# First rows of two experts loaded one step earlier in a fused HGRN2 and MoE kernel

## The chip, the cores and the metric

The kernel runs on one core of one Trainium2 chip. The time is the device time of one execution in microseconds, and the number given for a kernel is the median of several runs. A profiled execution gives the trace that is read here; its span is close to that time but not the same number.

The engines are named as in the profile: PE is TensorE (PEld its weight loads), DVE is VectorE, ACT is ScalarE, POOL is GpSimd, SP is SyncE, which here only issues DMAs.

## The reference

Two blocks follow one another. The first is a gated linear recurrence over 768 steps for 4 batches of 8 heads, with head size 48. The second is a mixture of 8 experts: each of the 3072 tokens goes to the one expert with the highest gate value, through a two-layer network of that expert, and is weighted by its gate probability. No token is dropped.

```python
# q, k, v, f_logit: (4, 8, 768, 48)
f = 1.0 / (1.0 + np.exp(-f_logit))
for t in range(S):
    state = f[:, :, t, :, None] * state + np.einsum('bhd,bhe->bhde', k[:, :, t], v[:, :, t])
    y[:, :, t] = np.einsum('bhd,bhde->bhe', q[:, :, t], state)
...
x = y.transpose(0, 2, 1, 3).reshape(3072, 384)
logits = x @ w_gate                    # (3072, 8)
expert_idx = np.argmax(logits, axis=1)
gate_w = softmax(logits)[arange, expert_idx]
...
for e in range(8):                     # rows of expert e
    h = np.maximum(x_sorted[lo:hi] @ w1[e], 0.0)     # w1: (8, 384, 1024)
    y_sorted[lo:hi] = h @ w2[e]                      # w2: (8, 1024, 384)
return gate_w[:, None] * y_sorted[inv_perm]
```

## The kernel before

**The recurrence.** It is cut into 12 units (NU = 12). A unit is one chunk of 128 time steps of two batches, all heads: 256 tokens. The loop at line 765 runs steps n = 1 to 13 as a software pipeline. In step n, unit n has its scores computed, unit n - 1 its output products, and unit n - 2 is copied out (`settle`), transposed together with the gate product (`rows`, tile `xp`, line 625) and laid into rows of a token-major tile `xr` (`lay`).

**Routing.** Finished units are routed in groups: [0,1], [2,3], [4,5], [6,7], [8,9], [10], [11]. `choose` finds each token's expert on VectorE. `count` is two small TensorE products (lines 220 and 221) that count tokens by expert. `place` (lines 227 to 245, VectorE) adds the counts to the running ends of the experts' regions and gives each token its row number `posi`. `fill` (lines 252 to 254) writes the gate weight. `send` then scatters the rows to the DRAM table `xs` by indirect DMAs from GpSimd (line 183), one for each 128 tokens. Each expert has its own region in `xs`, filled from its front in the order of routing. `settled` does place and fill, and queues the sends; a group of two units has four scatters, which go out two in each of the next two steps. `scatter_some` issues them. From step 10 on it issues all that are waiting: group [6,7] is settled in step 10 and its four scatters go out in that step, group [8,9] and [10] in step 12, group [11] in step 13.

**The early tiles.** Once an expert has 128 rows, its first full tile can be computed while the last units are still being routed. This is done for experts 0 and 1 (EARLY = 2). `load_rows` reads the tile from `xs` (four blocks at line 267, and the token numbers and gate weights `tg` at line 278, ten DMAs for the two experts, all on SyncE's queue). `turn` transposes it by VectorE (line 288). `widen` is the first layer on TensorE (line 304), with its ReLU on ScalarE (line 314) or VectorE (line 316), and `narrow` the second layer (line 320, tile `yp`), weighted by the gate at line 331 and scattered to the output. The tile of expert 0 is turned in step 12, and its first layer runs in pieces between the last products of the routing in steps 12 and 13. The tile of expert 1 follows after the loop.

**The test for full tiles.** If experts 0 and 1 do not have 128 rows each when the tile is loaded, the early tile would be wrong. Lines 713 to 720 therefore compare the running ends with `full` and write a flag `fix`, which at the end of the program would run a general loop over all experts (line 1106). The test is made when the group that is the last one before the loads is settled.

**Order.** All engines are under a hand-written order (`manual_schedule`): each engine runs its instructions in the order in which the program records them. The framework adds the waits for data. For `xs` it knows only the table as a whole: scatters do not wait for each other (they are declared free of conflicts), but a load of rows waits for every scatter recorded before it, and a scatter recorded after a load waits until that load has landed. A wait holds up everything behind it in its engine's own order, DMA issues on SyncE's queue too.

**After the loop**, the remaining rows of each expert are computed in tiles of up to 384 rows (`rows_of`, `narrow_late`), with rows beyond that collected in groups of four experts (`widen_quad`). The weights of expert 0 and 1 are loaded in steps 8 and 10 (lines 350 and 355), 1.5 MB for each tensor.

Of the kernel before, what the change touches and what calls it, by code (L numbers as in the profile page):

```python
# [25 lines left out]
NU = B // 2 * NC  # L26
# [28 lines left out]
EARLY = 2  # L55
# [64 lines left out]
def kernel(  # L120
# [22 lines left out]
    def const(name):  # L143
        a, w = fat[name]
        return fpack[:, a : a + w]
# [49 lines left out]
    class Route:  # L195
# [60 lines left out]
        def send(self, chunks):  # L256
            for c in chunks:
                scatter(xs, self.posi[:, c : c + 1], self.xr[:, c, :], ROWS - 1, self.group)
# [5 lines left out]
    def load_blocks(to, rows):  # L264

        for j in range(128 // BK):
            nc.sync.dma_start(
                to[BK * j : BK * j + BK],
                rows[:, DB * j : DB * j + DB].rearrange("(i c) m -> c i m", c=BK),
            )  # L270

    def load_rows(row, n=1):

        rows = xs[ds(row, n * C)] if not isinstance(row, int) else xs[row : row + n * C]
        x = rowp.tile([128, TILES * C // BK, DB], F32, name="xrow")[:, 0 : n * C // BK]
        tg = rowp.tile([128, TILES, USED - TOK], F32, name="tg")[:, 0:n]
        load_blocks(x, rows)
        nc.sync.dma_start(tg, rows[:, TOK:USED].rearrange("(t p) r -> p t r", p=C))
        return {"n": n, "x": x, "tg": tg}
# [58 lines left out]
    first = [e * REGION for e in range(E)]  # L338
# [44 lines left out]
    with ExitStack() as st:  # L383
# [85 lines left out]
        def by_r(u, part=whole, on=nc.gpsimd):  # L469
            k = units[u]["k"][:, part]  # L470
            ins = on.tensor_tensor(k, k, units[u]["r"][:, part], op=OP.mult).ins  # L471
            if routed:

                tc.add_manual_dep(ins, routed.pop().name, SYNC, reason="the port of both")

        def ends(u):
            nc.gpsimd.tensor_copy(rend[:, u], units[u]["sum"][:, :, C])
# [21 lines left out]
        def score(u, a):  # L499
            x = units[u]  # L500
            x["at"] = scores[u % 2]
            ps = x["ps", a] = [pss.tile([128, HP, C], F32, name="s") for h in range(2)]
            for p, h, r in heads():
                s = HP * a + p
                nc.tensor.matmul(  # L505
                    ps[h][:, p], lhsT=x["k"][r, s], rhs=x["q"][r, s], start=True, stop=True
                )
# [15 lines left out]
        def keep(u):  # L523
            for a in range(2):
                nc.scalar.copy(units[u]["kn"][:, HP * a : HP * a + HP], units[u]["kp"][a])  # L525
# [65 lines left out]
        def settle(u):  # L591
            x = units[u]
            x["ys"] = wk.tile([128, 2, HP, C], F32, name="ys", bufs=1)
            for a in range(2):
                nc.scalar.copy(x["ys"][:, a], x["yt"][:, a])  # L595
# [112 lines left out]
        def settled(n, rt):  # L708

            rt.place()  # L710
            rt.fill()
            lead["base"] = rt.after
            if n == NU - 3:
                lack = wk.tile([1, EARLY], F32, name="lack", bufs=1)
                some = wk.tile([1, 1], F32, name="some", bufs=1)
                nc.vector.tensor_tensor(
                    lack, rt.after[0:1, 0:EARLY], const("full")[0:1, 0:EARLY], op=OP.is_lt
                )
                nc.vector.reduce_max(some, lack, axis=AX_X)
                nc.vector.tensor_copy(fix, some)  # L720
            if n < NU:
                for c in range(0, rt.n, 2):
                    sends.append(lambda c=c: rt.send(range(c, c + 2)))
            else:
                rt.send(range(rt.n))
# [3 lines left out]
        def scatter_some(n):  # L729
            now = sends if n >= NU - 1 else sends[:1]  # L730
            for send in now:
                send()
            del sends[: len(now)]
# [31 lines left out]
        for n in range(1, NU + 2):  # L765
            here, back, last = n, n - 1, n - 2
            ahead = n + 1 < NU
            state = n < NU - 2
            rt = None
            if here < NU:  # L770
                units[here]["old"] = states[here % 2]
            if 1 <= last:
                settle(last)
            if later and later[0] < NU - 1:
                later[1].weigh()
            if here < NU:
                for a in range(2):
                    score(here, a)
            if ahead and n != 2:
                by_r(n + 1)  # L780
                ends(n + 1)
            if decayed:
                decayed()
                decayed = None
            if sends:
                scatter_some(n)
            if n == 1:
                units[0]["old"] = None
                added(0)
                update(0)()  # L790
            if ahead and n != 2:
                decay(n + 1)
                last_decay(n + 1)
            if state:
                keys(here)
                keep(here)
            if n == 2:
                growth(n + 1)
                by_r(n + 1)
                ends(n + 1)  # L800
                decay(n + 1)
                last_decay(n + 1)
            if here < NU:
                for a in range(2):
                    for h in range(2):
                        mask(here, a, h)
            if n == 1:
                log(3)
            if n + 3 < NU:
                steps(n + 3)  # L810
            if later and n >= NU - 1:
                settled(*later)
                later = None
                scatter_some(NU)
            if 2 < n < NU - 2:
                total(n + 2)
            if n == NU - 2:
                by_decay(n + 1)
            if 0 <= last:
                rt = rows(last, later[1] if later else None)  # L820
                lay(last)
            if later and n == NU - 2:
                settled(*later)
                later = None
                scatter_some(NU)
            if ahead and n < NU - 2:
                by_decay(n + 1)
            if n == 2:
                total(n + 2)
            if rt:  # L830
                rt.choose()
                if n < NU - 2:
                    routed.append(rt.latest)
                if n >= NU - 1:
                    rt.weigh()
            if later:
                settled(*later)
                routed.append(later[1].latest)
                later = None
            for a in range(2):  # L840
                if back < NU:
                    within(back, a)
            if n == 1:
                settle(0)
            if n + 2 < NU and n != 1:
                growth(n + 2)
            if n == NU + 1:
                widen(soon[0], weights[0], early_h, range(3, 7))
            if n == NU:
                turn_early(soon[0])  # L850
            if state:
                added(here)
                decayed = update(here)
            if n == 1:
                total(3)
            if back < NU:
                before(back)
            if rt:
                later = (n, rt)
                if n >= NU - 1:  # L860
                    rt.count(turns("rp", [128, 2, rt.n, E]))
                if n >= NU:
                    settled(*later)
                    later = None
            if n == NU:
                early_h = early_banks()
                widen(soon[0], weights[0], early_h, range(3))
            if n == NU + 1:
                widen(soon[0], weights[0], early_h, range(7, NF))
                turn(soon[1])  # L870
            if n == 1:
                load(n + 3, "q")
            if n + 3 < NU:
                load(n + 3, "k")
            if n + 2 < NU:
                load(n + 2, "v")
            if 1 < n and n + 3 < NU:
                load(n + 3, "q")
            if n + 5 < NU:
                load(n + 5, "f")  # L880
            if n == 1:
                load_first_pads()
            if n in (8, 10):
                load_first_weights((n - 8) // 2)
                load_second_weights((n - 8) // 2)
            if n == NU - 1:
                soon = [load_rows(first[e]) for e in range(EARLY)]


        def share():  # L890
# [368 lines left out]
```

## Time and profile before

| what | us |
|---|---|
| time, median of 3 runs | 409.92 (407.5 to 410.32) |
| span of the profiled execution | 410.9 |
| TensorE busy | 390.1 (95%) |
| VectorE busy | 170.6 (42%) |
| ScalarE busy | 102.9 (25%) |
| GpSimd busy | 112.3 (27%) |
| tiles of all experts, TensorE from 153.28 to 402.39 | 249.1 |

TensorE's share of 95% says that the kernel as a whole is bound by it, but the average hides that the stretches differ. The recurrence with its routing takes the first 130 us or so, then comes a short stretch in which routing ends and the early tiles run, and then the full tiles, which are nothing but matmuls. In the last part there is no wait left to take away. A wait in the middle stretch counts only if TensorE stands still for it.

Where the profile says "issue", the engine waited for nothing that the profile shows. "Remote" or "another core or an unknown queue" means that a semaphore changed at that time but the trace could not tie the change to the end of an instruction; on a kernel of one core it is not another core. In a windows table each engine has its busy time and its number of instructions, then follow the clock that was granted to TensorE (1.00 is full), the busy share of the DMA engines, and GB/s.

### The profile page before, as it was taken

Reading aid. Unit: us, or ns where it says so; the run is one execution under the profiler, and the core shown is the slowest. Engines: PE = TensorE matmul, PEld = TensorE weight load, DVE = VectorE, ACT = ScalarE, POOL = GpSimd, SP = SyncE. Lnnn points to the kernel's source line nnn. Section 1 sums busy time; section 2 is a strip of 40 time slices with the busy share of each in tenths; the row PEclk is TensorE's granted clock in tenths of the full one; section 3 lists DMA queues with packets and bytes.
Section 4 is the critical chain, followed back from the end, with each engine's and each line's share of the span. In section 5 each row is a group of like instructions: output and inputs, shape, how many; then the busy total and the mean of one; then the engine's idle time right before and its main releaser. Section 6 shows DMA issues by size and latency. Waiting matters only on the chain.

```text
span 410.9 us, 7299 instructions
## 1 busy us (share of the span) xinstructions
PE 390.1 (95%) x2870; PEld 272.1 (66%) x2870; DVE 170.6 (42%) x364; ACT 102.9 (25%) x190; POOL 112.3 (27%) x118
## 2 busy tenths in 40 slices
PE   7878999999999699999999999999999999999991
PEld 7878899989978478685555555545455555554540
DVE  6989888887752631212131131119112113111810
ACT  7888778675232001010100100110000000001000
POOL 5378667778705200000001001000200100100020
PEclk9998999999999699999999999999999999999997
DMA  8998667769953358785539999892172379994010
GB/s 291 406 359 296 213 213 256 237 200 360 404 156 105 121 157 282 176 294 109 185 108 396 362 384 332 322 352 31 51 255 83 97 252 383 405 406 169 1 46 17
DMA packets 52122, 95.22 MB, mean 232 GB/s; under 512 B 21440, under 2 KB 41333, under 8 KB 50032
## 3 DMA queue, kind: packets, MB, share of 16 engines
q1 hardware_dynamic: 48592, 84.96, 61.1%
q0 software_dynamic: 3200, 9.64, 6.3%
q8 instruction: 24, 0.39, 0.4%
q10 hardware_dynamic: 288, 0.08, 0.1%
q14 instruction: 18, 0.15, 0.1%
HBM read 79.65 MB, written 15.40 MB: 231 GB/s over the span
## 4 chain that ended last, share of the span: by engine, by line
PE 86%; DMA 4%; ACT 3%; DVE 2%; another core or an unknown queue 1%; issue 1%; SPq 0%; POOL 0%; POOLq 0%; ACTq 0%; DVEq 0%
PE yps L320 28%; PE hps L304 28%; PE xp L625 6%; PE yt L533 5%; PE s L505 4%; DMA f<-in_fu_dram 4%; PE yp L320 3%; PE yps L1059 3%; PE hps L1033 3%; PE yt L554 2%; PE s L304 2%; PE dp L570 2%; PE kp L520 1%; ACT g L438 1%
## 5 line engine op out<-in xcount | busy, mean ns | idle before, releaser
L320 PE MATMUL yps<-w2t,hT 128*128 128x384 f32 x352 | 115.6, 487 | 0.0
L304 PE MATMUL hps<-xT,w1t 128*128 128x384 f32 (+1 forms) x384 | 114.9, 459 | 0.0
L304 PEld LDWEIGHTS hps<-xT,w1t 128*128 128x128 f32 x384 | 73.0, 190 | 41.1
L320 PEld LDWEIGHTS yps<-w2t,hT 128*128 128x128 f32 x352 | 66.5, 190 | 48.1 <-issue 2.9
L183 POOL DMA_INDIRECT out_dram<-ysb,dst x26 | 25.3, 972 | 239.7 <-DVE ysb L331 239.4
L314 ACT ACTIVATE hT<-hps 128x384 f32<-128x384 f32 (+1 forms) x28 | 14.1, 505 | 209.7 <-PE hps L304 190.8
L316 DVE TENSOR_SCALAR hT<-hps 128x384 f32<-128x384 f32 (+1 forms) x28 | 16.2, 577 | 97.2 <-PE hps L304 97.2
L331 DVE TENSOR_SCALAR ysb<-yps,tg 128x384 f32<-128x384 f32 x22 | 13.6, 618 | 73.4 <-PE yps L320 73.4
L183 POOL DMA_INDIRECT xs<-xr,posi x24 | 30.9, 1289 | 22.3 <-issue 16.7
L511 DVE COPY_PREDICATED at<-mpack,s 128x512 f32<-128x512 uint8 x48 | 31.2, 727 | 11.9 <-PE s L505 10.3
L471 POOL TENSOR_TENSOR k<-k,r 128x1024 f32<-128x1024 f32 (+1 forms) x12 | 26.5, 2209 | 25.6 <-ACT r L467 9.9
L625 PE MATMUL xp<-fpack,ys 128*128 128x104 f32 x192 | 25.9, 286 | 4.6 <-ACT kn L525 3.7
L453 DVE TENSOR_TENSOR_SCAN sum<-g,cap 128x1032 f32<-128x1032 f32 (+1 forms) x14 | 28.7, 2051 | 2.7 <-ACT g L446 2.6
L625 PEld LDWEIGHTS xp<-fpack,ys 128*128 128x128 f32 x192 | 23.3, 196 | 6.9 <-ACT kn L525 4.9
L505 PE MATMUL s<-q,k 64*128 64x128 f32 x384 | 24.7, 278 | 1.6 <-POOL last L489 1.0
L533 PE MATMUL yt<-at,v 128*48 128x128 f32 x384 | 25.1, 282 | 0.6 <-issue 0.6
L505 PEld LDWEIGHTS s<-q,k 64*128 64x128 f32 x384 | 22.4, 188 | 3.5 <-issue 1.5
L533 PEld LDWEIGHTS yt<-at,v 128*48 128x48 f32 x384 | 21.3, 127 | 2.6 <-issue 1.6
L320 PE MATMUL yp<-w2t,hT 128*128 128x384 f32 x32 | 13.6, 584 | 3.3 <-DVE hT L316 3.3
L494 DVE TENSOR_TENSOR q<-q,g 128x1024 f32<-128x1024 f32 (+1 forms) x14 | 16.4, 1182 | 0.0
L595 ACT COPY ys<-yt 128x512 f32<-128x512 f32 x24 | 12.8, 587 | 13.8 <-PE yt L554 13.8
L288 DVE STREAM_TRANSPOSE xT<-xrow 128x1152 f32<-128x1152 f32 (+2 forms) x10 | 14.3, 1433 | 0.8 <-DMA xrow<-xs 0.7
(110 smaller groups left out, 324.6 us busy)
## 6 DMA issues: line engine op xcount, KB each, us to landing
qw<-in_moe_w_dram SPq DMA_DIRECT2D x16, 1536.0 KB
w1t<-in_moe_w_dram SPq DMA_DIRECT2D x8, 1536.0 KB
w2t<-in_moe_w_dram SPq DMA_DIRECT2D x8, 1536.0 KB
k<-in_ku_dram SPq DMA_DIRECT2D x12, 512.0 KB
q<-in_qu_dram SPq DMA_DIRECT2D x12, 512.0 KB
f<-in_fu_dram SPq DMA_DIRECT2D x11, 512.0 KB
xs<-pad SPq DMA_DIRECT2D x8, 600.0 KB
v<-in_vu_dram SPq DMA_DIRECT2D x12, 384.0 KB
```

Source lines behind the costliest of these rows:

```text
L183: ins = nc.gpsimd.indirect_dma_start(out=dst, out_offset=bass.IndirectOffsetOnAxis(ap=idx, axis=0), in_=src, in_offset=None, bounds_check= ...
L288: nc.vector.transpose(x["xT"].rearrange("p k (i c) -> p i k c", c=BK), x["x"].rearrange("p i (r k) -> p i k r", k=KD),)
L304: nc.tensor.matmul(x["h"][:, f], lhsT=w[0][:, j, b * 128 : b * 128 + 128], rhs=x["xT"][:, j], start=j == 0, stop=j == KD - 1,)
L316: nc.vector.tensor_scalar(to, x["h"], 0.0, None, op0=OP.max)
L320: nc.tensor.matmul(yp, lhsT=x["hT"][:, f, t * C : t * C + C], rhs=w[1][:, f, :], start=f == 0, stop=f == NF - 1,)
L453: nc.vector.tensor_tensor_scan(x["sum"][:, part].rearrange("p s c -> p (s c)"), x["g"][:, part].rearrange("p s c -> p (s c)"), cap[:, part ...
L471: ins = on.tensor_tensor(k, k, units[u]["r"][:, part], op=OP.mult).ins
L494: nc.vector.tensor_tensor(q, q, x["dec"][:, part], op=OP.mult)
L505: nc.tensor.matmul(ps[h][:, p], lhsT=x["k"][r, s], rhs=x["q"][r, s], start=True, stop=True)
L511: nc.vector.copy_predicated(x["at"][:, a, h], _bc(causal, 1, HP), x["ps", a][h])
L533: nc.tensor.matmul(x["yt"][DP * (h ^ a) : DP * (h ^ a) + D, a, p], lhsT=x["v"][:, a, 2 * p + h], rhs=x["at"][:, a, h, p], start=p == 0, st ...
L625: nc.tensor.matmul(xp[:, p], lhsT=x["ys"][:, a, p], rhs=wx[:, p, 0:XW] if a else wx[:, p, E:WX], start=True, stop=True,)
```

## The change

The loads of the first tiles of experts 0 and 1 move from the end of step 11 to the middle of step 10, right after that step's call of `scatter_some`. There the last scatters recorded before them are those of group [4,5], not [6,7]. So the test for full tiles, too, is taken one group earlier: with NU = 12, `n == NU - 3` is the group that is completed in step 9, [6,7], and `n == NU - 5` the one of step 7, [4,5]. The purpose is to issue the loads earlier, behind fewer scatters. The scatters of group [6,7], which stood before the loads in the program, now stand behind them, and so do the weight loads of expert 1 on SyncE's queue. TensorE, ScalarE and GpSimd have the same instructions in the same order as before; VectorE's three test instructions and SyncE's loads are the ones that move.

```diff
@@ settled(n, rt)
             lead["base"] = rt.after
-            if n == NU - 3:
+            if n == NU - 5:
                 lack = wk.tile([1, EARLY], F32, name="lack", bufs=1)
                 some = wk.tile([1, 1], F32, name="some", bufs=1)
                 nc.vector.tensor_tensor(
...
@@ the loop over n
             if sends:
                 scatter_some(n)
+            if n == NU - 2:
+                soon = [load_rows(first[e]) for e in range(EARLY)]
             if n == 1:
                 units[0]["old"] = None
                 added(0)
...
             if n in (8, 10):
                 load_first_weights((n - 8) // 2)
                 load_second_weights((n - 8) // 2)
-            if n == NU - 1:
-                soon = [load_rows(first[e]) for e in range(EARLY)]
```

## The prediction

> **What bounds the kernel now.** I read three views in this order: the chain of waits around the place of the change, the windows of that stretch, and the timelines of VectorE, the SyncE queue and GpSimd there. The chain first. From 153.28 us to 402.39 us it is TensorE alone (the windows give 249.08 us busy of 249.12), so nothing done before 150 us can help that part except by letting it start sooner. The only long piece of the chain that is not TensorE's after 37 us is this:
>
> ```profile
> 125.27 1.78 PE xp L625 x16
> 128.47 6.06 another core or an unknown queue
> 134.56 0.19 DVE counts L228
> 136.07 0.67 DVE hT L316
> 136.78 5.49 PE yp L320 x8
> ```
>
> The reader should see a VectorE instruction, the copy of group [11]'s counts at line 228, starting 6 us after its predecessor, then the place computation, then the hT that TensorE needs for the second half of `yp`. The windows show what this costs TensorE:
>
> ```profile
> core 0: us, PE busy (x) PEld busy (x) DVE busy (x) ACT busy (x) POOL busy (x), PEclk, DMA share, GB/s
> 109.20:115.00 5.80, 5.22 (x64) 4.32 (x60) 2.93 (x5) 0.72 (x2) 3.91 (x4) 1.00 1.04 390
> 130.69:133.44 2.75, 2.75 (x10) 1.33 (x8) 0.00 (x0) 0.00 (x0) 2.17 (x5) 1.00 0.41 149
> 133.44:136.78 3.34, 0.00 (x0) 0.00 (x0) 1.95 (x10) 0.00 (x0) 0.30 (x3) 0.86 0.16 61
> 136.78:142.69 5.91, 5.91 (x11) 3.48 (x12) 4.55 (x20) 0.00 (x0) 2.02 (x2) 0.50 0.52 176
> ```
>
> TensorE is idle for 3.34 us and then runs 5.91 us at a granted clock of 0.50. The timeline names the neighbours of that wait:
>
> ```profile
> 125.89 0.97 POOL L183 DMA_INDIRECT xs<-xr,posi  x1 [11.81 <-issue]
> 129.72 0.37 PE L221 MATMUL rp<-oh,fpack 128*128 128x16 f32 x2
> 132.51 0.97 POOL L183 DMA_INDIRECT xs<-xr,posi  x1 [0.31 <-issue]
> 133.60 0.14 POOL L617 MEMSET xr<- 128x28 f32 x1
> 134.56 0.17 DVE L228 COPY counts<-rp 128x16 f32<-128x16 f32 x1 [6.08 <-remote]
> ```
>
> The product that line 228 waits for has left TensorE at 130.09 (129.72 + 0.37). In the semaphore events kept in the trace, TensorE's increment for it arrives at 134.53, 4.4 us late. In that time GpSimd issues scatters one behind another: six from 125.89 to 133.48. The same lateness, 1.4 to 3.3 us, stands at 110.7 to 115.0, and there too GpSimd has a row of scatters (four, 109.27 to 114.08). Where it has only two together (95.33 and 96.68, for one) the increments come within 0.05 us. From one trace this is a coincidence in time, not a proven cause.
>
> Why six scatters stand together at 125.89: GpSimd was idle for 11.81 us before them, though the places of group [8,9] were ready at 119.2 (line 254: 119.01 + 0.18). The rows of `xs` that the early loads read must not be overwritten by a later scatter before they are read, so those scatters wait for all ten loads, and the loads came late:
>
> ```profile
> 99.91 0.46 SPq L350 DMA_DIRECT2D w1t<-in_moe_w_dram  x1
> 100.42 1.32 SPq L355 DMA_DIRECT2D w2t<-in_moe_w_dram  x1
> 118.35 1.76 SPq L267 DMA_DIRECT2D xrow<-xs  x4
> 120.63 2.44 SPq L267 DMA_DIRECT2D xrow<-xs  x4
> ```
>
> They were issued at 118.35, when the scatters of [6,7] (to 114.08) had landed, behind 3 MB of weights; they landed by 124.87.
>
> **What the Trainium skill says.** "DMA: Bandwidth & Descriptors", section Rules for kernel authors: a DMA that reads what an earlier one wrote must wait for that one's completion semaphore. The trace agrees: the queue waits 14.9 us at longest at line 267 for `xs<-xr,posi`. "Perfetto Trace Analysis", section DMA Instruction — SWDGE (GPSIMD): the recorded end of such a scatter is the end of descriptor generation, not of the movement. Agrees: 0.97 us recorded, 2.6 us at least to landing. "TensorE: Matmul & The Clock Gate", Part 1: an idle window of about 3.4 us halves TensorE's clock. Agrees: 3.34 us idle, then 0.50. The same page, section The cost: per-tile semaphore tail, gives 26.3 ns per increment; the 4.4 us here are nothing of that kind, so no price of the page covers them.
>
> **The change part by part.**
>
> *The test.* Three tiny VectorE instructions (lines 716, 719, 720: 0.12, 0.14 and 0.14 us, about 0.45 us with gaps) move from group [6,7], at 108.90, to group [4,5], at 91.6. There they precede the state addition of line 587 (0.54 us, whose next wait on TensorE has 1.34 us of idle time to absorb them). Cost nothing. The test asks whether experts 0 and 1 have 128 rows each by then. Counting the routing on the reference's inputs gives 238 and 207 after unit 5, so it still passes and the fallback loop stays unused; otherwise the kernel would be far slower.
>
> *The loads.* On the queue they now stand before the second expert's w1t and w2t and behind v, issued at 99.53. They wait for the second half of group [4,5]'s scatters, GpSimd 104.30 and 105.64. In the kernel before these landed at 111.26 and 112.35 among the weights' packets; those weights are now queued behind the loads. Low end: 2.6 us after 105.64, so 108.3; high end the old 112.35. I take 108.6. The ten loads then land 6.5 us later (118.35 to 124.87 before), at 115.1. They were needed at 121.07 (VectorE waits 0.74 us for them at line 288), so that wait goes, but behind it line 228 waits for TensorE's 123.17 in both kernels: worth 0.
>
> *The new wait.* Group [6,7]'s four scatters, issued at 109.27 before, must now wait for the loads: 115.1 plus the 1.02 us seen between 124.87 and 125.89, so 116.1. Behind them on GpSimd stand only scatters and the fills of lines 616 and 617; the last decay and state products are ahead of them. With one scatter each 1.28 us: [6,7] to 120.9, [8,9] to 126.0, [10] from 126.4 to 128.7. Before, [10] ended at 133.48. So GpSimd is behind by 7 us at first and ahead by 4.8 at the end. If the loads land only at 118.9 (high end), [10] ends at 132.5, still not later than before. Who waits for the scatters of [6,7]: ScalarE's first copy into the reused `xr` (126.41). With the old 5 to 7 us to landing under full queues they land at 125 to 127; ScalarE's hT at 128.54 has 1.5 us until TensorE's 130.69. Cost 0 to 0.5, taken as 0.
>
> *The weights.* Issued at 113.7 instead of 99.91. 3 MB plus scatters at some 390 GB/s end near 126; they are read after 136. Cost nothing.
>
> *The end of the stretch.* With the six-scatter row over at 128.7, before the product of 130.09, I expect its increment on time. VectorE needs 1.5 us from line 228 to line 316 (134.56 to 136.06) and 0.67 for it: hT is there at 132.3, before TensorE's first half ends at 133.44. The idle 3.34 us go. Without them the clock stays at 1.00, so the 5.91 us at 0.50 take about half: 2.95 saved. Sum 6.3. Next in line, the first full tile of expert 0, was turned at 149.57 for use at 153.28; its rows move up with VectorE's 4.4 us, and with TensorE at 147.0 about 1.9 us of slack remain (turn 143.9 to 145.1). So the whole 249 us block starts 6.3 us earlier. A small extra, 0.6 us of "issue" gaps of TensorE at 114.15 to 115.02 amid full DMA queues, may go too; I leave it out of the point.
>
> **The rivals.**
>
> *The late increment has another cause.* Then line 228 starts at 134.5 as before, the DMA work moved was hidden anyway, and the time is 409.9 (409 to 411). For it: only two such places in the trace, and the first is also one with full queues. Against: both fall in rows of four or more scatters.
>
> *The wait goes, part of it returns.* The row of scatters is now ten long, 116.1 to 128.7, over the products and copies of units 10 and 11. An increment late by 1.4 us is covered there (line 212's result at 120.98 is needed at 122.55: 1.57 us of slack), one by 3 us is not. One or two such stalls give 405.5 to 407.
>
> *Slower.* All increments from about 118 on are held to the end of the row, 129.7. TensorE then stops at the product of 122.55 until 131.2; the 10.9 us up to 133.44 and the 2.6 us of the second half follow, with about 2.5 us for half clock: 147.2 against 142.27. So 409.9 + 5 = 415. For it: the row of six held one for 4.4 us. Against: in both rows the first 0.6 to 1.8 us passed freely, and the row of four let one through every 1.4 us.
>
> **How the numbers follow.** Forecast, with the whole gain: 0.55; 409.92 - 3.34 - 2.95 = 403.6. Partial return 0.15, other cause 0.18, slower 0.12. With the extra of 0.6 and the scatter of runs (407.5 to 410.32) the low end is 401.8; the high end must reach past 409.9 to 411, leaving out the slower case. One per cent is 4.1 us: faster (under 405.8) 0.55 plus a little of the partial case, 0.58; slower (over 414) 0.10; the rest, 0.32, within.
>
> **What would show it.** Right: loads issued near 108.6; [6,7]'s scatters near 116; no VectorE wait of several us at line 228; no TensorE gap before the second half of `yp`; clock 1.00 through 142; the full tiles of expert 0 starting near 147. Wrong: waits at lines 633, 228 or 595 on TensorE between 118 and 130, or a half clock there; the old 6 us wait still standing; or the loop after the full tiles running, which would mean that the test fell.

## The result and the profile after

| kernel | median, us | lowest to highest | executions |
|---|---|---|---|
| before | 410.12 | 407.5 to 410.57 | 4 |
| after | 405.31 | 404.74 to 406.76 | 4 |

The ratio is 0.9898, with a 95% interval of 0.9855 to 0.994. Ratios here leave out executions in a second, slower state, and are not the quotients of the medians beside them. Two later measurements of the same changed kernel gave 0.9918 (0.9894 to 0.9942) both times. The change makes the kernel about 1% faster. The time that I predicted, 403.6 us, was 1.7 us too low.

Three of the four executions of before are the ones given above with the kernel before. These are the windows of the kernel after, in three of the stretches shown of before. The columns are as there: length, then TensorE's busy time and instructions first, the granted clock third from the end.

```profile
core 0: us, PE busy (x) PEld busy (x) DVE busy (x) ACT busy (x) POOL busy (x), PEclk, DMA share, GB/s
130.69:133.44 2.75, 2.75 (x13) 1.84 (x13) 2.47 (x13) 0.00 (x0) 1.02 (x4) 1.00 0.33 125
133.44:136.78 3.34, 3.34 (x14) 2.13 (x13) 3.03 (x15) 0.00 (x0) 1.62 (x2) 1.00 0.57 190
136.78:142.69 5.91, 5.91 (x51) 5.64 (x50) 1.79 (x7) 0.60 (x1) 0.97 (x1) 1.00 0.46 140
```

TensorE is busy in all three, at full clock. The chain of waits says the same: from 118.18 us to the end of the full tiles it is TensorE alone.

```profile
127.54 2.70 PE s L304 x24
130.24 0.13 PE rp L220 x2
130.37 0.22 PE rp L221 x2
130.59 0.76 PE s L304 x6
131.36 5.16 PE yp L320 x16
136.52 5.36 PE s L304 x48
...
147.26 10.36 PE hps L304 x48
```

The 6 us piece ahead of line 228 is gone, and `yp` is one piece of 16 products. The full tiles start at 147.26 in place of 153.28. The timelines show what was moved, SyncE's queue and GpSimd first, then VectorE:

```profile
110.74 1.76 SPq L267 DMA_DIRECT2D xrow<-xs  x4
...
116.02 0.43 SPq L350 DMA_DIRECT2D w1t<-in_moe_w_dram  x1
118.31 1.01 POOL L183 DMA_INDIRECT xs<-xr,posi  x1 [8.97 <-DVE counts L228]
...
130.07 0.97 POOL L183 DMA_INDIRECT xs<-xr,posi  x1 [0.30 <-ACT hT L314]
121.52 0.70 DVE L288 STREAM_TRANSPOSE xT<-xrow 128x384 f32<-128x384 f32 x1
...
130.63 0.17 DVE L228 COPY counts<-rp 128x16 f32<-128x16 f32 x1 [1.64 <-PE rp L221]
```

The loads are issued at 110.74 and the weights after them. Ten scatters run from 118.31 to 131.04. Expert 0's row is turned at 121.52 without a wait, and group [11]'s counts (line 228) come 0.04 us after their product, whose end the trace puts at 130.59.

One thing did not fit at once. By the prediction's reading a row of GpSimd scatters holds TensorE's increments back. Here the row is ten long, and each of TensorE's increments in the trace comes within 0.05 us of the end of its product. So a row alone does not cause the lateness, and the gain needed another look.

### The profile page after: what moved, and what is told of

The parts are those of the page before. It is cut to its first block, busy times and chain, and to the rows that moved or that the text cites. A ratio compares the mean times of both kernels' runs of the same rounds, so it can differ in the third digit from the quotient of the medians.

```text
span 404.9 us, 7298 instructions
## 1 busy us (share of the span) xinstructions
PE 386.6 (95%) x2870; PEld 270.7 (67%) x2870; DVE 170.6 (42%) x364; ACT 102.9 (25%) x190; POOL 111.5 (28%) x118
## 4 chain that ended last, share of the span: by engine, by line
PE 88%; ACT 3%; DVE 3%; DMA 2%; POOL 1%; issue 1%; SPq 0%; POOLq 0%; DVEq 0%; ACTq 0%
PE yps L320 28%; PE hps L304 28%; PE xp L625 6%; PE yt L533 5%; PE s L505 4%; PE s L304 3%; PE yps L1059 3%; PE hps L1033 3%; PE yp L320 3%; PE yt L554 3%; PE dp L570 2%; DMA f<-in_fu_dram 2%; ACT kn L525 1%; DVE sum L453 1%; DVE q L494 1%; PE kp L520 1%
## 5 line engine op out<-in xcount | busy, mean ns | idle before, releaser
L533 PE MATMUL yt<-at,v 128*48 128x128 f32 x384 | 23.8, 277 | 0.0
L438 ACT ACTIVATE g<-f 128x1024 f32<-128x1024 f32 (+1 forms) x14 | 13.2, 941 | 4.1 <-DMA f<-in_fu_dram 4.1
```

What stands on the lines that cost most here:

```text
L533: nc.tensor.matmul(x["yt"][DP * (h ^ a) : DP * (h ^ a) + D, a, p], lhsT=x["v"][:, a, 2 * p + h], rhs=x["at"][:, a, h, p], start=p == 0, st ...
```

## The experiments

Four theories are named in the expectations. *Increment* is the prediction's: in the kernel before, TensorE's increments come late in the row of six scatters, which holds VectorE and then TensorE. *Queue* was its first rival: the lateness is an accident of one execution, or a GpSimd fill behind the scatters is what waits. *Program* and *Execution* (later *Chip*) ask whether lateness goes with the kernel's program or with where and when it runs. *Load*, formed after the second group of runs, says that TensorE waits for VectorE's turn of expert 0's first row (line 288), because the loads wait for the scatters of [6,7] to land. The kernels ran in three groups of four. Each group ran on one chip, and each on a different one.

The table gives all twelve. "Stretch" runs from the start of group [4,5]'s third scatter (104.30 in the kernel before) to the start of the first full-tile product (153.11 there), both read from the timelines; on it the kernel before had 48.81 us and the kernel after 40.95. "Late" says whether TensorE's increments come over 1 us late between 105 and 140 us.

| group, kernel | median, us | ratio to before (95%) | stretch, us | late |
|---|---|---|---|---|
| 1 before again | 409.2 | 1.0006 (0.9984 to 1.0028) | 45.33 | yes |
| 1 loads only | 416.08 | 1.0181 (1.0117 to 1.0245) | 50.52 | TensorE itself stutters |
| 1 weights later | 408.49 | 0.9988 (0.9957 to 1.0019) | 43.19 | yes |
| 1 fill on VectorE | 408.67 | 0.9984 (0.9957 to 1.0011) | 46.11 | yes |
| 2 after again | 406.29 | 0.9918 (0.9894 to 0.9942) | 40.95 | no |
| 2 loads only again | 406.52 | 0.9917 (0.9885 to 0.9949) | 40.94 | no |
| 2 test only | 409.4 | 1.0001 (0.9979 to 1.0023) | 44.98 | no |
| 2 loads only, spaced | 408.41 | 0.9992 (0.9974 to 1.001) | 42.68 | no |
| 3 weights later again | 405.72 | 0.9933 (0.9908 to 0.9957) | 41.27 | no |
| 3 expert 0 early | 409.67 | 1.0012 (0.999 to 1.0034) | 43.59 | no |
| 3 widen later | 409.31 | 0.9996 (0.9976 to 1.0016) | 44.67 | no |
| 3 after, third time | 405.27 | 0.9918 (0.9894 to 0.9942) | 41.19 | no |

### Group 1: is the late increment real, and what sets it?

**Kernel before again**, no edit.

> The kernel before, unchanged, in a second profiled execution. Two theories of the stall before the second half of yp. Theory Increment: TensorE's semaphore increment for the counts of group [11] is what comes late, so line 228 starts about 134.5 again, some 4 us after the product. Theory Queue: the increment was an accident of that one execution, and what is there each time is GpSimd's late row of six scatters, which keeps the fill of group [11]'s xr (lines 616 and 617) to about 133.7; VectorE's reciprocal at line 254 waits for that fill and hT stands behind it. Then line 228 starts near 130.1, line 254 near 133.8, and TensorE is idle 1.1 to 1.5 us instead of 3.3. Time 410 in both.

The increments are late again: products that end at 131.89 and 132.66 have theirs at 134.03 and 136.93 in the semaphore events kept in the trace. VectorE and TensorE wait, in the timelines:

```profile
134.06 0.18 DVE L228 COPY counts<-rp 128x16 f32<-128x16 f32 x1 [3.79 <-PE s L304]
...
136.95 0.69 DVE L316 TENSOR_SCALAR hT<-s 128x512 f32<-128x512 f32 x1 [1.30 <-remote]
137.70 2.85 PE L320 MATMUL yp<-w2t,hT 128*128 128x384 f32 x8 [2.46 <-DVE hT L316]
```

So it was no accident of one execution. This time 2.46 us of idle were not followed by a half clock; why is taken up further down.

**Loads only**: the changed kernel with the test left where it was.

```diff
-            if n == NU - 5:
+            if n == NU - 3:
```

> The loads moved as in the changed kernel, the test for full tiles left with group [6,7]. Both theories: the whole gain, 405 (404.5 to 406.5); the test's three VectorE instructions of 0.12 to 0.14 us are worth nothing. If the test's place matters, it is slower than the changed kernel by up to 0.5 us.

It came out slower than before, against both theories. TensorE stuttered in the products of line 554, which wait for nothing that the profile shows, and a half clock followed. Timeline of TensorE, then two windows:

```profile
120.37 0.43 PE L554 MATMUL yt<-q,state 48*48 48x128 f32 x7
...
122.61 0.43 PE L554 MATMUL yt<-q,state 48*48 48x128 f32 x4 [0.45 <-issue]
124.03 0.68 PE L554 MATMUL yt<-q,state 48*48 48x128 f32 x4 [0.98 <-issue]
125.46 0.68 PE L554 MATMUL yt<-q,state 48*48 48x128 f32 x4 [0.75 <-issue]
126.88 1.10 PE L554 MATMUL yt<-q,state 48*48 48x128 f32 x5 [0.75 <-issue]
```

```profile
120.40:129.00 8.60, 4.51 (x35) 1.89 (x33) 0.25 (x3) 0.00 (x0) 5.18 (x8) 0.65 1.01 366
129.00:133.50 4.50, 4.50 (x23) 4.50 (x23) 1.31 (x8) 1.07 (x2) 0.98 (x1) 0.53 0.03 10
```

Four or five products pass every 1.4 us while eight scatters run (116.93 to 126.85) and the DMA engines are full (share 1.01). All four executions took 414.6 to 417.5 us.

**Weights later**: the kernel before, with expert 1's weights loaded after the early rows in step 11.

```diff
-            if n in (8, 10):
-                load_first_weights((n - 8) // 2)
-                load_second_weights((n - 8) // 2)
+            if n == 8:
+                load_first_weights(0)
+                load_second_weights(0)
             if n == NU - 1:
                 soon = [load_rows(first[e]) for e in range(EARLY)]
+                load_first_weights(1)
+                load_second_weights(1)
```

> The kernel before with one edit: expert 1's w1t and w2t are loaded after the early rows instead of before them; the rows still wait for group [6,7]'s scatters. These then land 2.6 us after their last issue at 113.1 instead of at 118.2, so the loads go out near 116, land near 122.5, and the six scatters with the fills behind them end near 131.3 instead of 133.7. Theory Queue: hT is there before TensorE's first half ends, no idle time, no half clock: 405 to 406, all of the gain without moving behind another group. Theory Increment: the row of six is still there over the product at 130.1, whose increment is held to about 132: idle 0.5 to 1.5 us, 407 to 409.

Late increments stay (a product that ends at 127.13 has its increment at 130.63), TensorE loses 1.05 us ahead of `yp`, and the median does not move.

**Fill on VectorE**: the kernel before, with the fills of `xr` for [10] and [11] on VectorE.

```diff
-                nc.gpsimd.tensor_copy(group["xr"][:, :, TOK], toks)
-                nc.gpsimd.memset(group["xr"][:, :, USED:ROW], 0.0)
+                on = nc.vector if u >= NU - 2 else nc.gpsimd
+                on.tensor_copy(group["xr"][:, :, TOK], toks)
+                on.memset(group["xr"][:, :, USED:ROW], 0.0)
```

> The kernel before with one edit: the fills of xr (lines 616 and 617) of groups [10] and [11] run on VectorE instead of GpSimd, so the reciprocal at line 254 no longer waits for what stands behind the scatters. Loads and scatters stay where they were. Theory Queue: hT comes at 132.3 plus 0.4, no idle time, clock stays full: 405 to 406.5. Theory Increment: line 228 still waits to about 134.5, and the time stays at 410.

A product that ends at 130.57 has its increment at 134.53 and TensorE waits 2.15 us for hT. The fills are not the cause, and theory Queue fell. After this group Increment stood, with the slow loads-only kernel as a riddle: it differs from the kernel after by the place of three VectorE instructions.

### Group 2: which half of the change gains, and is it the program?

**After again**, no edit.

> The changed kernel once more, in the same session as the three runs beside it. Theory Program (whether TensorE is held during the row of scatters belongs to the program): 405 +- 1.5 us, ratio 0.985 to 0.995, every increment of TensorE within 0.1 us of the end of its product between 118 and 131 us. Theory Execution (the first run of it was a lucky one, since the loads alone lost): 408 to 416 us, with increments 1 to 4 us late or gaps in the row of 32 products of line 554.

**Loads only again**, the edit of group 1.

> The loads of the first rows in unit 10's step, the test for full tiles left where it was, as before. Theory Program: 416 +- 1.5 us again, with TensorE's gaps of 0.4 to 1 us in line 554 while eight scatters run. Theory Execution: nearer 405 in some of its executions, no gaps in the profile.

**Test only**: the kernel before with `n == NU - 5` for the test alone.

```diff
-            if n == NU - 3:
+            if n == NU - 5:
```

> The other half alone: the test for full tiles two groups earlier, the loads where they were. The prediction prices the test at nothing, so theory Increment expects the time of the kernel before, ratio 0.995 to 1.005, with TensorE's increments late in the two rows of scatters. A theory under which the place of the three VectorE instructions decides whether increments come in time expects 404 to 406 us, ratio about 0.99, and increments in time.

**Loads only, spaced**: two GpSimd fills ahead of each of the eight scatters of [6,7] and [8,9]. The expectation names [10] too, but the edit leaves its two scatters without fills.

```diff
...
             for c in chunks:
+                if spacer is not None:
+                    for _ in range(2):
+                        nc.gpsimd.memset(spacer, 0.0)
                 scatter(xs, ...)
...
```

> The loads alone, with two GpSimd fills of an unused 128x512 tile (an estimate of 0.9 us for the two, from the 1.8 us that a fill of 128x2048 took) ahead of each of the scatters of groups [6,7] to [10]. The row of eight then takes about 8 x 2.2 = 18 us in place of 10. Theory Row (TensorE is held because the scatters follow each other without a break): the gaps in line 554 go, the clock stays whole, and the time falls from 416 towards 405 to 408, less what the later scatters of [10] and [11] cost. Theory that the row isn't the cause (the loads' or the weights' transfers are): gaps stay at 120 to 129 us and the time at 416 or above.

On this chip the halves separate cleanly: the loads alone have the whole gain (406.52 us, against 406.29 with both halves), the test alone has none. The stutter of group 1 is not in the loads-only program: the same kernel took 416.08 us on the first chip and 406.52 on this one. No kernel of this group has late increments, and this is what overturned my theory. The test-only kernel keeps the order of scatters of the kernel before, the row of six included, all its increments come in time, and it still takes the time of before. With a ratio of 1.0001 it stands for the kernel before, of which there is no profile on this chip. Its profile shows where the time goes when nothing is late. Timelines of SyncE's queue, VectorE, TensorE, then windows:

```profile
118.37 1.76 SPq L267 DMA_DIRECT2D xrow<-xs  x4
123.15 0.69 DVE L288 STREAM_TRANSPOSE xT<-xrow 128x384 f32<-128x384 f32 x1 [3.59 <-DMA xrow<-xs]
123.90 3.75 PE L304 MATMUL s<-xT,w1t 128*128 128x128 f32 x18 [2.24 <-DVE xT L288]
```

```profile
121.66:123.90 2.24, 0.01 (x1) 0.00 (x0) 0.75 (x4) 0.65 (x2) 0.00 (x0) 1.00 0.26 44
123.90:128.00 4.10, 4.10 (x22) 4.10 (x23) 1.27 (x9) 0.00 (x0) 1.01 (x2) 0.58 0.13 26
```

The loads leave at 118.37, VectorE waits 3.59 us for them, TensorE 2.24 us for VectorE, and then runs 3.41 us at half clock, which costs half of that, 1.7 us. Why they leave so late is in the chain of the same kernel: the last scatter of [6,7] needs 5.27 us to land. Expert 1's 3 MB of weights, issued at 99.76 and 100.30, are a likely reason: the DMA engines are full (share 1.01 from 109 to 116 us). The next group tests it.

```profile
111.67 0.97 POOL xs L183
112.64 0.30 issue
112.95 5.27 DMA xs<-xr,posi
...
118.37 0.34 SPq L267
```

The sum, 2.24 + 1.7 = 3.9 us, is the difference of the stretches, 44.98 - 40.95 = 4.03 us. The spans differ by less, 406.9 - 404.5 = 2.4 us, because the after run lost 1.6 us in the start-up, where no edit acts: its scatter of [4,5] started at 105.77, this one's at 104.15. The reason is in the clock: TensorE ran at half clock from 40.91 to 44.32 us in the after run, and at full clock until 124.43 here. A half clock of that length costs 1.7 us, so single spans can differ by this much without any edit.

Of the test-only kernel's 20 executions two took 2273 us. Neither was traced. The general loop behind `fix` is a suspect, but no run shows that it ran. None of the 19 executions of the kernel after took so long, and none of the 20 of expert 0 early in group 3; both make the test at the same place.

The spaced kernel tells nothing on the row, since the unspaced one did not stutter here. It lost 1.9 us against the unspaced one. The scatters of [11] ran to 139.41, and the first full tile was not turned in time:

```profile
146.99 3.26 PE L307 MATMUL hps<-xT,w1t 128*128 128x256 f32 x14 [1.26 <-DVE dst L296]
```

### Group 3: Load against Increment

**Weights later again**, the edit of group 1.

> Kernel before with expert 1's w1t and w2t loaded after the early rows in step 11, once more, now beside other kernels. The scatters of [6,7] and the loads then don't share the queues with 3 MB of weights, so the first row is turned near 121.1 us, before TensorE asks for it. Theory Load (TensorE waits 2.2 us for the turn of expert 0's first row because the loads wait for the landing of [6,7]'s scatters): the gain of the changed kernel, ratio 0.99, 405.5 to 407 us, unless increments are late. Theory Increment (increments held in the row of six scatters): six scatters in a row stay, so the time of before, ratio 0.997 to 1.003, and in the profile increments 1 us or more late between 126 and 134 us.

Without late increments it has the gain, with the loads still in step 11. Now the last scatter of [6,7] is issued at 113.24 and lands at 115.83, after 2.59 us in place of 5.27. The DMA share from 109 to 116 us is 0.33 where it was 1.01. The window of the test-only kernel and then of this one:

```profile
109.00:116.00 7.00, 6.98 (x112) 6.28 (x110) 3.96 (x13) 2.41 (x7) 3.91 (x4) 1.00 1.01 382
109.00:116.00 7.00, 7.00 (x116) 6.41 (x114) 4.39 (x17) 2.42 (x7) 3.90 (x4) 1.00 0.33 119
```

Timelines of SyncE's queue, VectorE, TensorE:

```profile
115.98 1.76 SPq L267 DMA_DIRECT2D xrow<-xs  x4
119.77 0.70 DVE L288 STREAM_TRANSPOSE xT<-xrow 128x384 f32<-128x384 f32 x1
121.81 2.25 PE L304 MATMUL s<-xT,w1t 128*128 128x128 f32 x18
```

The row is turned at 120.47 for use at 121.81, and no wait is left. The stretch is 41.27 us, close to the 40.95 of the kernel after. The four scatters from 123.91 and the two of [10] from 129.24 are still close together. So the landing of [6,7]'s scatters beside the weights is what held the loads, and with them TensorE.

**Expert 0 early**: expert 0's row in step 10, expert 1's in step 11.

```diff
             if n == NU - 2:
-                soon = [load_rows(first[e]) for e in range(EARLY)]
+                soon = [load_rows(first[0])]
...
+            if n == NU - 1:
+                soon.append(load_rows(first[1]))
```

> The change with half of the loads: expert 0's row in unit 10's step, expert 1's in step 11 as before (test as in the change). The scatters of [8,9] still wait for expert 1's loads, so the row of six scatters stays near 126 us as before. Theory Load: all of the gain, 406 us, ratio 0.99. Theory Increment, by way of the row of six at [10] and [11]: no gain, 409 us, ratio 0.997 to 1.003.

Load's number missed: there was no gain. The trace says why. VectorE's turn, TensorE's wait for it, and the late end, from the timelines:

```profile
121.18 0.71 DVE L288 STREAM_TRANSPOSE xT<-xrow 128x384 f32<-128x384 f32 x1
123.21 2.25 PE L304 MATMUL s<-xT,w1t 128*128 128x128 f32 x18
131.46 0.97 POOL L183 DMA_INDIRECT xs<-xr,posi  x1 [10.43 <-DVE su L252]
148.11 1.20 DVE L288 STREAM_TRANSPOSE xT<-xrow 128x768 f32<-128x768 f32 x1 [4.90 <-DMA xrow<-xs]
149.46 4.72 PE L304 MATMUL hps<-xT,w1t 128*128 128x256 f32 x14 [2.50 <-DVE dst L293]
```

The wait for the first row is gone, as Load said (no gap at 123.21). But [6,7]'s scatters now went out beside the weights and landed at 126.69, expert 1's loads waited for them (issued 126.83), and [8,9]'s scatters for those loads. So the last scatters ended at 142.13, and the first full tile came 2.50 us late with a half clock after it: one wait of that size in place of the other. So all ten loads must be done early, since the later scatters wait for the last of them.

**Widen later**: TensorE's first 18 products on expert 0's row go behind the 16 of line 625.

```diff
-            if n == NU:
-                early_h = early_banks()
-                widen(soon[0], weights[0], early_h, range(3))
...
             if n == NU + 1:
-                widen(soon[0], weights[0], early_h, range(3, 7))
+                early_h = early_banks()
+                widen(soon[0], weights[0], early_h, range(7))
```

> Kernel before with nothing moved on the queues: TensorE's first 18 products of line 304 on expert 0's row go behind the 16 of line 625 for unit 11, in place of ahead of them. Theory Load: TensorE's wait of 2.24 us ahead of line 304 (123.90) falls to the 0.7 us until ScalarE's copy of line 595 is there (122.3), the half clock of 3.4 us after it goes, and the time is 405.5 to 407, ratio about 0.99. Theory Increment: no gain, 409, ratio 0.997 to 1.003.

A miss again for Load's number, though not for the load wait itself:

```profile
124.61 0.69 DVE L288 STREAM_TRANSPOSE xT<-xrow 128x384 f32<-128x384 f32 x1 [3.46 <-DMA xrow<-xs]
...
125.77 0.17 DVE L239 TENSOR_TENSOR place<-rp,sums 128x16 f32<-128x16 f32 x1
126.09 1.61 PE L625 MATMUL xp<-fpack,ys 128*128 128x104 f32 x8 [1.49 <-DVE place L239]
```

I had thought of TensorE's wait alone. VectorE's 3.46 us at line 288 hold all that stands behind it there, and TensorE's second half of line 625 needs group [10]'s place computation (line 239). The wait went from 2.24 to 1.49 us, the half clock of 3.41 us stayed.

**After, third time**, no edit.

> The changed kernel beside these three. Both theories expect 405 to 407.6 us, ratio 0.99. If increments are late in the profiles of the other three, as they were in the first four runs, theory Chip (lateness belongs to the chip or the hour, not to the program) expects them late here too in the row of ten scatters, 118 to 131 us; theory Program expects them in time here all the same.

405.27 us, nothing late, but nothing was late beside it either, so Chip and Program stay undecided for this kernel: it was not among the four of group 1.

## Why the prediction was right, and where it was wrong

- **The bound and the place of the gain: right.** All of it is TensorE's standing still, and running at half clock, between 105 and 150 us; the full tiles after that only start sooner. Taken by spans, it is 410.9 - 404.9 = 6.0 us in the two profiles first compared, of 6.3 predicted; by the medians of the same measurement it is 410.12 - 405.31 = 4.8 us.
- **The test costs nothing: right.** 1.0001 (0.9979 to 1.0023) alone.
- **The moves: right within 2.4 us.** Loads at 110.74 (108.6 predicted; the scatters they wait for were issued 1.85 us later than before, for reasons of the start-up, and landed at 110.55), the [6,7] scatters at 118.31 (116.1), row's end 131.04 (128.7), hT ready at 132.8 (132.3), full tiles 147.26 (147.0). ScalarE's first copy into the reused `xr` and the weights cost nothing, as said.
- **The step that failed: "The loads".** It says that VectorE's wait of 0.74 us for them goes, "but behind it line 228 waits for TensorE's 123.17 in both kernels: worth 0". In that one trace TensorE was itself held up earlier, where late increments stood (from 112.60 us on its 32 products of line 533 took 3.3 us, against 1.96 in test only), and came to line 304 at 123.02, just after the row was ready. In the test-only kernel, where nothing is late, it is there at 121.66, and the wait that I priced at 0 is worth 2.24 + 1.7 = 3.9 us, nearly the whole difference of the stretches there (4.03).
- **"The end of the stretch" held the wrong cause.** Its 3.34 + 2.95 = 6.3 us were real in the trace that it was read from, but the row of six does not have to hold increments: with test only it did not. Nor does a row of ten in the kernel after. Where nothing is late, the gain is 2.7 to 4.0 us by the medians of groups 2 and 3 (408.96 - 406.29, 409.27 - 405.27), not 6.3. The point was 1.7 us too low, and this is a likely reason. The traced execution that the 6.3 was read from took 412.75 us, 2.8 us more than the median of 409.92 that it was taken off.
- **What was luck.** One and the same move ended two different waits: the one priced at 6.3 us, which is not there in every execution, and the one priced at 0, which is worth 3.9 us where the first is missing. That either one brings the time into the stated range was not foreseen, and in so far the range held by luck.
- **The rivals.** "The late increment has another cause" was right in its premise and wrong in its time: with that cause gone, the transfer was still worth moving. "Slower" did not come in the kernel after, but its picture, TensorE held through a long row of scatters, is what the loads-only kernel showed on the first chip, with 1.018.

The Trainium skill, "TensorE: Matmul & The Clock Gate", Part 1, which the prediction used, gives an idle window of about 3.4 us as what halves the clock. The prediction's trace agreed (3.34 us). These runs do not: 1.49, 2.24 and 2.50 us of idle were each followed by 3.41 us of half clock (widen later, test only, expert 0 early), while 2.46 us (before again) and 1.26 us (loads only, spaced) were not. The length of the half clock is the page's window. A wait of 1.5 to 2.5 us can thus cost 1.7 us more than itself.

Why 2.24 us may have done it and 2.46 us not can be read from the clock record. There the granted clock changes only at the edges of a grid of 3.41 us (the pieces of the kernel before last 3.41, 6.83 and 102.40 us, for three), so it matters how much of one grid step is idle. The step that holds the idle and the one after it, first of test only, then of before again:

```profile
121.02:124.43 3.41, 1.17 (x12) 1.05 (x9) 1.21 (x6) 1.07 (x2) 0.00 (x0) 1.00 0.29 57
124.43:127.85 3.42, 3.42 (x19) 3.42 (x17) 0.81 (x6) 0.00 (x0) 0.97 (x1) 0.50 0.09 16
133.32:136.73 3.41, 1.92 (x6) 0.77 (x5) 1.31 (x8) 0.00 (x0) 2.55 (x7) 1.00 0.40 148
136.73:140.15 3.42, 2.45 (x8) 1.53 (x9) 3.03 (x10) 0.00 (x0) 1.69 (x2) 1.00 0.41 152
```

TensorE was busy for 1.17 us of its step in the first, and the clock was halved in the next. In the second the 2.46 us lie across an edge, and 1.92 and 2.45 us of the two steps were busy. The other stalls fit: 0.98 us busy (before), 1.27 (fill on VectorE), 1.36 (expert 0 early) and 1.72 (widen later) were followed by a half clock. Near half a step it goes either way: in the start-up 1.71 us was followed by one in the kernel after and by none in weights later again. The stutter of loads only does not fit, with 2.20 us busy ahead of its half clock. This is a reading of these traces, not an experiment on it.

What stays open: why increments were late, and TensorE held, in all four kernels of group 1 and in the first profile of before, but not in the first profile of after, nor in any of the eight kernels on the two other chips. Chip and hour can't be told apart here. The recording may have a part in it: for the semaphore that most of TensorE's products increment, the five late or stuttering traces hold 242 to 244 increments and the nine others 245 or 246. That is untested. The before kernel's medians, 408.81, 408.96 and 409.27 us on the three chips, show no price of it; weights later (408.49 against 405.72) and loads only (416.08 against 406.52) do. Whether the kernel after keeps its gain under that condition was not measured.

## What to carry to other kernels

A load that reads what scatters wrote is issued only when the last of them has landed, so record it behind the fewest scatters that it needs, and keep bulk weights from between them: either of the two alone gave about 1% here, where no increment was late. Before pricing a wait at nothing because its engine is late anyway, ask whether that lateness is there in every execution. A second profile of the unchanged kernel did not answer it here, since the increments were late again; the profile of a twin that should cost nothing, on another chip, did. A wait taken from TensorE comes back through an in-order VectorE or a later scatter unless what stands behind the waiting instruction is freed too.

## What the runs showed of the hardware

- One and the same kernel differed by 9.6 us (416.08 and 406.52) between two groups of runs on two chips, with TensorE letting four or five products through every 1.4 us beside back-to-back scatters and full DMA queues on the first, and none of this on the second.
- A scatter of 128 rows landed 2.59 us after its issue with a DMA share of 0.33 around it, and 5.27 us after it beside 3 MB of weights, with a share of 1.01; in the after kernel's row of ten the first took 6.97 us (117.98 to 124.95 in the second group's run).
